# Layer norm transposes by DMA, from one SBUF tile to another, in place of TensorE

## The chip, the cores and the metric

The kernel runs on one core of a Trainium2 chip. The metric is the time on the device in microseconds (us), the median of several runs. One core has TensorE (in the profile PE, its weight loads PEld), VectorE (DVE), ScalarE (ACT), GpSimd (POOL) and SyncE (SP), and 16 DMA engines. DMAs are issued from the queues of SyncE and ScalarE.

## The reference

Two layers; each is a sliding-window attention block (32 heads of 32, a window of 8 keys two apart) and a gated MLP, with a layer norm before each block. All tensors are bfloat16, 2048 tokens of 1024.

```python
x = A_x
x = x + A(layernorm(x), A_wqkv, A_wo)         # q,k,v = x @ wqkv; 8 dilated keys per query; @ wo
x = x + B(layernorm(x), B_w1, B_w3, B_w2)     # (silu(x @ w1) * (x @ w3)) @ w2, inner size 3584
x = x + A(layernorm(x), A_wqkv, A_wo)
x = x + B(layernorm(x), B_w1, B_w3, B_w2)
```

## The kernel before

The tokens are cut into four chunks of 512. For each layer a chunk goes through a stage Q (layer norm, then q, k, v), two stages T (attention, nearly all on VectorE, with the `po` matmuls at the end) and a stage B (layer norm, then the MLP). The stages of different chunks are interleaved, so that TensorE works on B while VectorE works on T. A framework orders each engine's instructions when the program is built, from its own model of time. In the traces each engine keeps to that order: an instruction at the head of its queue that takes long delays all behind it.

The matmuls want the normalized rows with the feature dimension on partitions. So each layer norm of a chunk ends in transposes, 16 times in all (8 chunks for Q, 8 for B), with four row tiles each:

```python
    xnp = ctx.enter_context(tc.tile_pool(name="xn", bufs=2))
    psQ = ctx.enter_context(tc.tile_pool(name="psQ", bufs=2, space=PSUM))   # Q: two PSUM buffers
    psB = ctx.enter_context(tc.tile_pool(name="psB", bufs=4, space=PSUM))   # B: four
    # ... cut ...
    def ln_chunk(c, psum):
        with hp():                                     # high priority in the ordering
            # ... cut: statistics on VectorE, square root on ScalarE ...
            for j in range(TPC):                       # 4 row tiles of 128 x 1024
                xn = xnp.tile([P, D], BF16, name="xn")
                nc.vector.tensor_scalar(xn[:], x_sb[:, n, :], mv[:, j, 0:1], rstd[:, j:j + 1],
                                        op0=ALU.subtract, op1=ALU.mult)
                pT = psum.tile([P, KT, P], BF16, name="pT", tag="mm")
                for kk in range(KT):                   # 8 transposes of 128 x 128
                    nc.tensor.transpose(pT[:, kk, :], xn[:, kk * P:(kk + 1) * P], ident[:])
                nc.scalar.copy(xnT[:, :, j * P:(j + 1) * P], pT[:])
```

ScalarE also takes every result of Q out of PSUM, and applies silu to every gate of B:

```python
                    for kk in range(KT):               # Q: one PSUM buffer is filled in 8 matmuls
                        nc.tensor.matmul(ps[:], lhsT=w[:, kk, t::KT], rhs=xnT[:, kk, :], ...)
                    nc.scalar.copy(sgt[:, t - t0, :], ps[:])
                # ... cut; B:
                        nc.scalar.activation(sg[:], pg[:], ACTF.Silu)
                        nc.vector.tensor_tensor(hT[:, g0 + fi - f0, :], sg[:], pu[:], op=ALU.mult)
```

Of the kernel before, what the change touches and what calls it, by code (L numbers as in the profile page):

```python
# [15 lines left out]
def kernel(  # L16
# [13 lines left out]
    nc = tc.nc  # L30
    cfg = dict(cfg or {})
    P = 128
# [30 lines left out]
    const = ctx.enter_context(tc.tile_pool(name="const", bufs=1))  # L63
    wA = ctx.enter_context(tc.tile_pool(name="wA", bufs=2))
    wF = ctx.enter_context(tc.tile_pool(name="wF", bufs=4))
    xnp = ctx.enter_context(tc.tile_pool(name="xn", bufs=2))
    xtp = ctx.enter_context(tc.tile_pool(name="xnT", bufs=2))
    scr = ctx.enter_context(tc.tile_pool(name="scr", bufs=2))
    wk = ctx.enter_context(tc.tile_pool(name="wk", bufs=1))
# [6 lines left out]
    psQ = ctx.enter_context(tc.tile_pool(name="psQ", bufs=2, space=PSUM))  # L76
    psB = ctx.enter_context(tc.tile_pool(name="psB", bufs=4, space=PSUM))
# [22 lines left out]
    def hp(on=True):  # L100
        return tc.high_priority(offset=BOOST) if on else nullcontext()

    def ln_chunk(c, psum):
        with hp():
            xnT = xtp.tile([P, KT, CH], BF16, name="xnT")
            st = small.tile([P, TPC, 2, 6], FP32, name="st")
            mv = small.tile([P, TPC, 2], FP32, name="mv")
            for j in range(TPC):
                n = c * TPC + j
                for hh in range(2):  # L110
                    nc.vector.bn_stats(st[:, j, hh, :], x_sb[:, n, hh * 512:(hh + 1) * 512])  # L111
                nc.vector.bn_aggr(mv[:, j, :], st[:, j, :, :])
            sd = small.tile([P, TPC], FP32, name="sd")
            rstd = small.tile([P, TPC], FP32, name="rstd")
            nc.scalar.activation(sd[:], mv[:, :, 1], ACTF.Sqrt, bias=epst[:])
            nc.vector.reciprocal(rstd[:], sd[:])
            for j in range(TPC):
                n = c * TPC + j
                xn = xnp.tile([P, D], BF16, name="xn")
                nc.vector.tensor_scalar(xn[:], x_sb[:, n, :], mv[:, j, 0:1], rstd[:, j:j + 1],  # L120
                                        op0=ALU.subtract, op1=ALU.mult)
                pT = psum.tile([P, KT, P], BF16, name="pT", tag="mm")
                for kk in range(KT):
                    nc.tensor.transpose(pT[:, kk, :], xn[:, kk * P:(kk + 1) * P], ident[:])  # L124
                nc.scalar.copy(xnT[:, :, j * P:(j + 1) * P], pT[:])  # L125
        return xnT
# [6 lines left out]
    pending_ln = {}  # L133

    def q_stage(l, c, ln_next=None):
        xnT = pending_ln.pop((l, c), None)
        if xnT is None:
            xnT = ln_chunk(c, psQ)
        for which in range(3):
            w = wA.tile([P, KT, D], BF16, name="wqkv", tag="wA")  # L140
            nc.sync.dma_start(w[:], wqkv_v[:, :, which * D:(which + 1) * D])
            if l == 0 and c == 0:
                if which == 0 and NCH > 1:
                    nc.sync.dma_start(x_sb[:, TPC:2 * TPC, :], xin[:, TPC:2 * TPC, :])
                if which == 2:
                    for cc in range(2, NCH):
                        nc.sync.dma_start(x_sb[:, cc * TPC:(cc + 1) * TPC, :], xin[:, cc * TPC:(cc + 1) * TPC, :])
                    nc.sync.dma_start(wo[:], wo_v)
            for t0 in range(0, KT, SG):
                sgt = stg.tile([P, SG, CH], BF16, name="sgt")  # L150
                for t in range(t0, t0 + SG):
                    ps = psQ.tile([P, CH], FP32, name="ps", tag="mm")
                    for kk in range(KT):
                        nc.tensor.matmul(ps[:], lhsT=w[:, kk, t::KT], rhs=xnT[:, kk, :],  # L154
                                         start=(kk == 0), stop=(kk == KT - 1))
                    nc.scalar.copy(sgt[:, t - t0, :], ps[:])  # L156
                nc.sync.dma_start(qkv_d[l][which][:, t0:t0 + SG, c * CH:(c + 1) * CH], sgt[:])
            if which == 1 and ln_next is not None:
                pending_ln[ln_next] = ln_chunk(ln_next[1], psQ)

    def t_stage(l, tcx):
        tok0 = tcx * TCH
# [66 lines left out]
            nc.vector.tensor_tensor(xs, xs, ps[:].rearrange("p a b -> p (a b)"), op=ALU.add)  # L229

    def b_stage(c, last):
        xnT = ln_chunk(c, psB)
        for (f0, f1) in fsplits:
            for g0 in range(f0, f1, FG):
                gn = min(FG, f1 - g0)
                w1t = wF.tile([P, KT, FG * P], BF16, name="w1t", tag="wF")
                nc.sync.dma_start(w1t[:, :, 0:gn * P], w1_v[:, :, g0 * P:(g0 + gn) * P])
                w3t = wF.tile([P, KT, FG * P], BF16, name="w3t", tag="wF")
                nc.sync.dma_start(w3t[:, :, 0:gn * P], w3_v[:, :, g0 * P:(g0 + gn) * P])
                for fi in range(gn):  # L240
                    pg = psB.tile([P, CH], FP32, name="pg", tag="mm")
                    for kk in range(KT):
                        nc.tensor.matmul(pg[:], lhsT=w1t[:, kk, fi * P:(fi + 1) * P], rhs=xnT[:, kk, :],  # L243
                                         start=(kk == 0), stop=(kk == KT - 1))
                    pu = psB.tile([P, CH], FP32, name="pu", tag="mm")
                    for kk in range(KT):
                        nc.tensor.matmul(pu[:], lhsT=w3t[:, kk, fi * P:(fi + 1) * P], rhs=xnT[:, kk, :],  # L247
                                         start=(kk == 0), stop=(kk == KT - 1))
                    with hp():
                        sg = sgp.tile([P, CH], BF16, name="sg")  # L250
                        nc.scalar.activation(sg[:], pg[:], ACTF.Silu)  # L251
                        nc.vector.tensor_tensor(hT[:, g0 + fi - f0, :], sg[:], pu[:], op=ALU.mult)  # L252
            lastsplit = (f1 == fsplits[-1][1])
            for hh in range(2):
                w2ts = []
                for g0 in range(f0, f1, 8):
                    gn = min(8, f1 - g0)
                    w2t = wF.tile([P, 8, 512], BF16, name="w2t", tag="wF")
                    nc.sync.dma_start(w2t[:, 0:gn, :], w2_v[:, g0:g0 + gn, hh * 512:(hh + 1) * 512])
                    w2ts.append(w2t)  # L260
                for j in range(TPC):
                    n = c * TPC + j
                    acc = psB.tile([P, 512], FP32, name="acc", tag="mm")
                    for f in range(f0, f1):
                        nc.tensor.matmul(acc[:], lhsT=hT[:, f - f0, j * P:(j + 1) * P],  # L265
                                         rhs=w2ts[(f - f0) // 8][:, (f - f0) % 8, :],
                                         start=(f == f0), stop=(f == f1 - 1))
                    xs = x_sb[:, n, hh * 512:(hh + 1) * 512]
                    with hp():
                        nc.vector.tensor_tensor(xs, xs, acc[:], op=ALU.add)  # L270
                    if last and lastsplit:
                        nc.sync.dma_start(xout[:, n, hh * 512:(hh + 1) * 512], xs)
# [11 lines left out]
    for idx, (kind, l, c) in enumerate(stages):  # L284
        if kind == "Q":
            nxt = None
            if l == 0:
                for k2, l2, c2 in stages[idx + 1:idx + 2 + R]:
                    if k2 == "Q" and l2 == 0:
                        nxt = (l2, c2)  # L290
                        break
            q_stage(l, c, nxt)
        elif kind == "T":
            t_stage(l, c)
        else:
            b_stage(c, last=(l == 1))
# [30 lines left out]
```

## Time and profile before

| | before |
|---|---|
| time, median | 1697.18 us (1696.16 to 1697.53, 3 runs) |
| span of the profiled run | 1695.1 us |
| TensorE busy | 1653.8 us (98%) |
| VectorE / ScalarE busy | 1142.0 / 377.5 us |
| TensorE transposes | 512, 37.8 us busy |

The first lines are from the page. Behind an engine stand its busy time, its share of the span and its instructions; PEclk is the clock granted to TensorE in 40 slices, in tenths; q1 is SyncE's DMA queue, with packets, megabytes and share of the 16 engines' time.

```profile
span 1695.1 us, 19718 instructions
...
PE 1653.8 (98%) x7936; PEld 820.2 (48%) x7936; DVE 1142.0 (67%) x1926; ACT 377.5 (22%) x557; POOL 1.9 (0%) x12
...
PEclk9999999999999999999999999999999999999999
...
q1 hardware_dynamic: 282752, 288.25, 52.6%
```

The groups of instructions of the same page: line, engine, operation, tiles and shapes, count, then busy time, mean ns of one, idle time of the engine just before them, and what ended most of it.

```profile
L154 PE MATMUL ps<-xnT,wqkv 128*128 128x512 bf16 x1536 | 341.8, 382 | 5.8 <-ACT sgt L156 3.6
...
L225 PE MATMUL po<-wo,oT 128*128 128x512 bf16 x512 | 126.9, 380 | 7.7 <-DVE oT L131 6.6
L125 ACT COPY xnT<-pT 128x1024 bf16<-128x1024 bf16 x64 | 61.6, 1023 | 159.7 <-PE pT L124 155.0
...
L124 PE MATMUL pT<-ident,xn 128*128 128x128 bf16 x512 | 37.8, 225 | 23.4 <-DVE xn L120 20.7
```

The waits view (who waited for whom: us in total, times, longest).

```profile
PE pT L124 <- DVE xn L120: 20.7, 11, 11.7
...
PE po L225 <- DVE oT L131: 6.6, 13, 2.1
...
PE ps L154 <- ACT sgt L156: 3.6, 5, 1.8
```

One line of TensorE's timeline (start, duration), just before a Q stage of the second layer: sixteen transposes in 1.06 us.

```profile
917.38 1.06 PE L124 MATMUL pT<-ident,xn 128*128 128x128 bf16 x16
```

And the windows view for the first 250 us, in which most of layer 0's Q chunks fall. It is used as a clock later on: TensorE executed 1124 matmuls, 160 of them transposes, so 964 useful ones. (Busy time and count of each engine, then the granted clock, the DMA share and GB/s.)

```profile
core 0: us, PE busy (x) PEld busy (x) DVE busy (x) ACT busy (x) POOL busy (x), PEclk, DMA share, GB/s
0.00:250.00 250.00, 226.94 (x1124) 139.27 (x1125) 207.60 (x366) 87.51 (x135) 1.89 (x12) 0.99 0.73 245
```

### The profile page before, as it was taken

The numbers are of one execution on the slowest core, as the hardware profiler recorded it, in microseconds if no ns is written. First come the engines' busy times: TensorE is split into PE (matmuls) and PEld (weight loads), VectorE is DVE, ScalarE is ACT, GpSimd is POOL, SyncE is SP. The second block draws the span as 40 slices with busy tenths as digits, with TensorE's granted clock in tenths as the row PEclk, the third lists the DMA queues.
The fourth block names the chain that finished last, engine by engine and source line by source line (L and its number), as shares of the span: only waits on it lengthen the run. The fifth ranks groups of instructions, "written<-read, shape, count | busy, mean of one in ns | idle before, by whom it ended". The sixth has DMA issues, their size and how long they took to land.

```text
span 1695.1 us, 19718 instructions
## 1 busy us (share of the span) xinstructions
PE 1653.8 (98%) x7936; PEld 820.2 (48%) x7936; DVE 1142.0 (67%) x1926; ACT 377.5 (22%) x557; POOL 1.9 (0%) x12
## 2 busy tenths in 40 slices
PE   6999999999999999999999999999999999999999
PEld 4655644444444444564445644455444554444444
DVE  5599999999997822229982299823997159952212
ACT  3333422112212111132012320223212231121100
POOL 0000000000000000000000000000000000000000
PEclk9999999999999999999999999999999999999999
DMA  8975656553553344575344764357543555436442
GB/s 298 316 263 187 205 176 188 171 163 115 176 162 127 98 153 156 166 240 179 125 136 149 237 187 126 124 180 244 175 141 108 183 165 165 149 103 195 149 149 99
DMA packets 282843, 289.51 MB, mean 171 GB/s; under 512 B 6144, under 2 KB 256000, under 8 KB 282624
## 3 DMA queue, kind: packets, MB, share of 16 engines
q1 hardware_dynamic: 282752, 288.25, 52.6%
q8 instruction: 62, 1.02, 0.2%
q14 instruction: 29, 0.24, 0.0%
HBM read 258.87 MB, written 29.36 MB: 170 GB/s over the span
## 4 chain that ended last, share of the span: by engine, by line
PE 49%; DVE 42%; issue 4%; DMA 3%; ACT 2%; SPq 0%; DVEq 0%; ACTq 0%
PE acc L265 15%; PE pu L247 11%; PE pg L243 10%; PE ps L154 10%; DVE pr L177 6%; DVE tm L218 6%; DVE hT L252 4%; DVE pr L129 4%; PE po L225 3%; DVE tm L129 3%; DVE st L111 3%; DVE pr L130 2%; DVE tm L130 2%; DMA qkv_d_1_134<-sgt 2%; DVE x_sb L270 1%
## 5 line engine op out<-in xcount | busy, mean ns | idle before, releaser
L247 PE MATMUL pu<-xnT,w3t 128*128 128x512 bf16 x1792 | 429.9, 379 | 0.0
L243 PE MATMUL pg<-xnT,w1t 128*128 128x512 bf16 x1792 | 429.4, 379 | 0.3 <-ACT xnT L125 0.3
L265 PE MATMUL acc<-w2t,hT 128*128 128x512 bf16 x1792 | 392.7, 379 | 0.8 <-DVE hT L252 0.8
L154 PE MATMUL ps<-xnT,wqkv 128*128 128x512 bf16 x1536 | 341.8, 382 | 5.8 <-ACT sgt L156 3.6
L251 ACT ACTIVATE sg<-pg 128x512 bf16<-128x512 f32 x224 | 133.7, 597 | 676.9 <-PE pg L243 663.8
L154 PEld LDWEIGHTS <-wqkv 128*128 128x128 bf16 x1536 | 220.1, 144 | 120.2 <-issue 12.4
L265 PEld LDWEIGHTS <-hT 128*128 128x128 bf16 x1792 | 174.9, 98 | 209.6 <-DVE hT L252 1.5
L243 PEld LDWEIGHTS <-w1t 128*128 128x128 bf16 x1792 | 175.2, 98 | 208.2 <-issue 0.8
L247 PEld LDWEIGHTS <-w3t 128*128 128x128 bf16 x1792 | 175.2, 98 | 207.5
L177 DVE TENSOR_TENSOR pr<-qT,kT 128x2048 bf16<-128x2048 bf16 x128 | 154.0, 1217 | 170.8 <-DMA kT<-qkv_d_1_134 156.9
L252 DVE TENSOR_TENSOR hT<-sg,pu 128x512 bf16<-128x512 bf16 x224 | 152.4, 680 | 168.5 <-PE pu L247 160.4
L270 DVE TENSOR_TENSOR x_sb<-x_sb,acc 128x512 bf16<-128x512 bf16 x128 | 87.2, 682 | 147.6 <-PE acc L265 147.6
L156 ACT CAST sgt<-ps 128x512 bf16<-128x512 f32 x192 | 111.9, 585 | 229.4 <-PE ps L154 202.2
L218 DVE TENSOR_TENSOR tm<-At,vT 128x2048 bf16<-128x2048 bf16 x128 | 152.9, 1217 | 0.1
L225 PE MATMUL po<-wo,oT 128*128 128x512 bf16 x512 | 126.9, 380 | 7.7 <-DVE oT L131 6.6
L125 ACT COPY xnT<-pT 128x1024 bf16<-128x1024 bf16 x64 | 61.6, 1023 | 159.7 <-PE pT L124 155.0
L225 PEld LDWEIGHTS <-oT 128*128 128x128 bf16 x512 | 48.8, 97 | 89.8 <-DVE oT L131 39.3
L129 DVE TENSOR_TENSOR pr<-pr 128x1024 bf16<-128x1024 bf16 x128 | 86.4, 681 | 0.0
L129 DVE TENSOR_TENSOR tm<-tm 128x1024 bf16<-128x1024 bf16 x128 | 84.7, 684 | 0.0
L111 DVE BATCH_NORM_STATS2 st<-x_sb 128x6 f32<-128x512 bf16 x128 | 80.7, 672 | 4.7 <-DMA x_sb<-in_A_x_dram 4.4
L124 PE MATMUL pT<-ident,xn 128*128 128x128 bf16 x512 | 37.8, 225 | 23.4 <-DVE xn L120 20.7
L229 DVE TENSOR_TENSOR x_sb<-x_sb,po 128x1024 bf16<-128x1024 bf16 x32 | 38.8, 1212 | 24.5 <-PE po L225 24.4
(175 smaller groups left out, 511.2 us busy)
## 6 DMA issues: line engine op xcount, KB each, us to landing
w1t<-in_B_w_dram SPq DMA_DIRECT2D x56, 1024.0 KB, 5.4
w3t<-in_B_w_dram SPq DMA_DIRECT2D x56, 1024.0 KB, 7.4
wqkv<-in_A_wqkv_dram SPq DMA_DIRECT2D x24, 2048.0 KB, 9.0
w2t<-in_B_w_dram SPq DMA_DIRECT2D x48, 1024.0 KB, 5.5
w2t<-in_B_w_dram SPq DMA_DIRECT2D x16, 512.0 KB, 5.3
qkv_d_0_130<-sgt SPq DMA_DIRECT2D x16, 256.0 KB, 5.1
qkv_d_1_131<-sgt SPq DMA_DIRECT2D x16, 256.0 KB, 5.5
qT<-qkv_d_0_130 SPq DMA_DIRECT2D x8, 512.0 KB, 4.7
```

The source lines that it names most:

```text
L111: nc.vector.bn_stats(st[:, j, hh, :], x_sb[:, n, hh * 512:(hh + 1) * 512])
L129: nc.vector.tensor_tensor(buf[:, 0:4, :], buf[:, 0:4, :], buf[:, 4:8, :], op=ALU.add)
L154: nc.tensor.matmul(ps[:], lhsT=w[:, kk, t::KT], rhs=xnT[:, kk, :], start=(kk == 0), stop=(kk == KT - 1))
L156: nc.scalar.copy(sgt[:, t - t0, :], ps[:])
L177: nc.vector.tensor_tensor(pr[:], qT[:], kT[:, :, k0:k0 + TCH], op=ALU.mult)
L218: nc.vector.tensor_tensor(tm[:], At[:], win, op=ALU.mult)
L225: nc.tensor.matmul(ps[:, hh, :], lhsT=oT[:, t, j * P:(j + 1) * P], rhs=wo[:, t, hh * 512:(hh + 1) * 512], start=(t == 0), stop=(t == KT - 1))
L243: nc.tensor.matmul(pg[:], lhsT=w1t[:, kk, fi * P:(fi + 1) * P], rhs=xnT[:, kk, :], start=(kk == 0), stop=(kk == KT - 1))
L247: nc.tensor.matmul(pu[:], lhsT=w3t[:, kk, fi * P:(fi + 1) * P], rhs=xnT[:, kk, :], start=(kk == 0), stop=(kk == KT - 1))
L251: nc.scalar.activation(sg[:], pg[:], ACTF.Silu)
L252: nc.vector.tensor_tensor(hT[:, g0 + fi - f0, :], sg[:], pu[:], op=ALU.mult)
L265: nc.tensor.matmul(acc[:], lhsT=hT[:, f - f0, j * P:(j + 1) * P], rhs=w2ts[(f - f0) // 8][:, (f - f0) % 8, :], start=(f == f0), stop=(f == ...
```

## The change

The intent: TensorE is the limit, and transposes do no arithmetic, so let the DMA engines do them. A DMA transpose reads `xn` and writes `xnT` directly, without PSUM and without ScalarE's eviction (the copy out of PSUM). ScalarE's queue issues it: the issue is an instruction of ScalarE that starts the DMA, and the DMA has landed when all its data is in place. Only the first chunk, on whose layer norm everything waits, stays on TensorE. One more `xn` buffer covers the longer life of a tile.

```diff
-    xnp = ctx.enter_context(tc.tile_pool(name="xn", bufs=2))
+    xnp = ctx.enter_context(tc.tile_pool(name="xn", bufs=3))
@@ ln_chunk
+                if psum is None:
+                    nc.scalar.dma_start_transpose(out=xnT[:, :, j * P:(j + 1) * P], in_=xn[:])
+                    continue
                 pT = psum.tile([P, KT, P], BF16, name="pT", tag="mm")
@@ q_stage
-            xnT = ln_chunk(c, psQ)
+            xnT = ln_chunk(c, psQ if (l, c) == (0, 0) else None)
...
-                pending_ln[ln_next] = ln_chunk(ln_next[1], psQ)
+                pending_ln[ln_next] = ln_chunk(ln_next[1], None)
@@ b_stage
-        xnT = ln_chunk(c, psB)
+        xnT = ln_chunk(c, None)
```

## The prediction

> **What bounds the kernel now.** TensorE. The page's busy table gives PE 1653.8 us of a span of 1695.1 (98%); the granted clock is 0.999. Start to start (timeline view) the 512-column matmuls follow each other every 216 ns (128 acc matmuls in 27.6 us), so the 7,424 useful ones need 1603.6 us. The other 91 us: 11.7 before the first PE instruction, 3.6 after the last matmul, 42 of transposes (512, start to start 81 ns each, gaps included; 37.8 by the groups table), 8 of gaps just before transposes, the rest waits for buffers and VectorE, 16 of them before the po matmuls (their oT comes from VectorE, 97 to 100% busy from 100 to 500 us in the windows view).
>
> **Removed.** 480 of 512 PE transposes and their weight loads: on PE 480 x 81 ns = 39 us, plus some 6 us of waits before and between them (PE waiting for xn, 20.7 us by the waits view, mostly at the start, which stays). Also 60 ScalarE evictions of 1.02 us (ScalarE is 22% busy: worth nothing directly) and pT's turns in the PSUM pools.
>
> **Added.** 60 DMA transposes of 256 KB, 15.7 MB on top of 289.5 MB (5%). The Trainium skill, "DMA: Bandwidth & Descriptors", section "Latency and other measured facts", gives 261 GB/s for a transpose with a non-contiguous middle dimension: 1.0 us of data, an estimate. No run here shows a transpose yet; plain 256 KB stores in this trace land 3.3 to 5.5 us after issue, so I expect 3 to 6 us to land, some 15 us for a chunk's four, with only three xn buffers. Each holds ScalarE's queue while issued: SyncE's plain issues take 0.37 to 0.67 us; I estimate 1 us, what the eviction took.
>
> **Moved.** Transposes no longer wait for PSUM or PE. In the second layer the first two xn of a Q chunk are ready 20 to 100 us before they are transposed (893 against 917 us): most landing time will be hidden. xn[3] must wait for xn[0]'s landing, and VectorE works in order: waits of 1 to 3 us per chunk.
>
> **How much is critical.** Nearly all of the PE time removed, since PE is the limit: at most 45 us. I give back: in 100 to 500 us VectorE is as full as PE, so the 96 transposes there (about 10 us) mostly become longer waits of po for oT; elsewhere a few us of queue waits. Net gain 30 to 40 us.
>
> **Prediction.** 1661 us (-2.1%), 8 in 10 between 1643 and 1692. Faster by over 2%: 0.52; within 2%: 0.38; slower by over 2%: 0.10.
>
> **What would show it.** Right: PE busy about 1618 us; pT only 32 transposes; no PE wait longer than 2 us on xnT's DMA after the first chunk; po's waits grow by 5 to 10 us; DMA share up 1 to 4 points; ScalarE busy down about 60 us; no PE wait for weights.
>
> **What would make it wrong.** (a) The transpose is several times slower than the estimate, or slows the loads beside it: then PE waits for weights or xnT. (b) Issuing it, or waiting for xn, holds ScalarE's queue for several us: sg and sgt evictions come late, and with two PSUM buffers in Q and four in B, PE stops after 2 to 4 us; its issue times would show that. (c) VectorE stops for the third or fourth xn buffer in the T stage. (d) The new order of instructions places po worse or better: 10 us either way, unrelated to the transposes' cost.

## The result, and the profile after

The changed kernel is correct and takes 1717.37 us (1715.94 to 1718.16, 4 runs), against 1696.82 us (1696.16 to 1697.53) of the kernel before beside it. The ratio is 1.012, with a 95% interval of 1.0106 to 1.0134. Here and below, a ratio is the mean time of one kernel's fast runs over that of the other's fast runs of the same rounds, so it is not quite the ratio of the medians quoted. The change makes the kernel 20.5 us (1.2%) slower; 36 us faster was predicted.

| | before | after |
|---|---|---|
| span of the profiled run | 1695.1 us | 1716.0 us |
| TensorE busy | 1653.8 us | 1634.3 us |
| TensorE waits for ScalarE's `sgt` | 3.6 us | 30.7 us |
| VectorE waits for a landing, to reuse `xn` | none | 74.6 us |
| transposes on TensorE | 512 | 32 |

The page's lines after (q10 is ScalarE's DMA queue):

```profile
span 1716.0 us, 18813 instructions
...
PE 1634.3 (95%) x7456; PEld 795.2 (46%) x7456; DVE 1142.5 (67%) x1926; ACT 326.7 (19%) x502; POOL 1.9 (0%) x12
...
PEclk9898999999999999999999999999999999999999
...
q1 hardware_dynamic: 282752, 288.25, 52.7%
q10 hardware_dynamic: 63360, 15.74, 5.0%
```

The groups that answer to those of before, and the one that makes `xn`:

```profile
L246 PE MATMUL pg<-xnT,w1t 128*128 128x512 bf16 x1792 | 431.5, 380 | 11.5 <-ACT sg L254 11.5
...
L157 PE MATMUL ps<-xnT,wqkv 128*128 128x512 bf16 x1536 | 346.3, 387 | 31.8 <-ACT sgt L159 30.7
...
L228 PE MATMUL po<-wo,oT 128*128 128x512 bf16 x512 | 127.9, 380 | 15.5 <-DVE oT L134 12.2
...
L120 DVE TENSOR_SCALAR xn<-x_sb,mv,rstd 128x1024 bf16<-128x1024 bf16 x64 | 32.9, 543 | 75.3 <-DMA xnT<-xn 74.6
```

TensorE has 480 instructions fewer and is still later. Its idle time before the `ps` matmuls of stage Q (L157, formerly L154) rose from 5.8 to 31.8 us, and ScalarE's eviction ended nearly all of it. The clock dips in slices of the first 250 us. The waits view gives the same names, and a new one, VectorE waiting for the DMA that still reads an `xn` buffer:

```profile
DVE xn L120 <- DMA xnT<-xn: 74.6, 22, 7.6
...
PE ps L157 <- ACT sgt L159: 30.7, 6, 10.5
...
PE po L228 <- DVE oT L134: 12.2, 13, 1.9
...
PE pg L246 <- ACT sg L254: 11.5, 6, 4.0
```

What holds ScalarE? The view of the tile `xnT` shows the issues themselves (minimum, median and maximum ns that one held the queue) and the time to landing:

```profile
L123 ACTq DMA_TRANSPOSE xnT<-xn x60: 1246/1329/6813, 24.0 to 1532.3; - x60
...
DMA to landing us min/median/max: 3.1/6.4/11.9
```

An issue holds ScalarE's queue for 1.25 us at the least and 6.81 us at the most. Of the 60, 24 take over 2 us, mostly the second and third of a chunk; the first of a chunk never does (1.25 to 1.33 us in all 15), even where its own DMA lands only 11.9 us later. In the trace all 60 sum up to 139.7 us. ScalarE's timeline at the layer norm of the third chunk shows what that does:

```profile
66.75 0.58 ACT L159 CAST sgt<-ps 128x512 bf16<-128x512 f32 x1 [2.14 <-DMA qkv_d_2_132<-sgt]
67.47 11.62 ACTq L123 DMA_TRANSPOSE xnT<-xn  x3
79.14 1.07 ACT L159 CAST sgt<-ps 128x512 bf16<-128x512 f32 x2 [11.81 <-DMA xnT<-xn]
79.94 1.31 ACTq L123 DMA_TRANSPOSE xnT<-xn  x1
```

Three transposes are issued in a row and hold the queue from 67.47 to 79.09 us (1.25, 6.81 and 3.50 us). Their `xn` tiles had been written before, so it is not VectorE that ScalarE waits for. For 11.8 us no PSUM buffer is emptied. TensorE meanwhile:

```profile
65.77 3.51 PE L157 MATMUL ps<-xnT,wqkv 128*128 128x512 bf16 x15
79.78 5.71 PE L157 MATMUL ps<-xnT,wqkv 128*128 128x512 bf16 x13 [10.50 <-ACT sgt L159]
```

It fills what buffers it has, stops for 10.50 us, and then does 13 matmuls in 5.71 us, where the 15 ahead of the stop took 3.51. The granted clock has dropped to half (0.51 in the windows view of these 5.71 us, the third figure from the end):

```profile
79.78:85.49 5.71, 5.71 (x14) 2.30 (x14) 5.45 (x13) 1.02 (x2) 0.00 (x0) 0.51 0.68 165
```

The Trainium skill, "TensorE: Matmul & The Clock Gate", section "Why this matters for your kernels", tells to avoid idle gaps of more than about 3 us for that reason; this trace agrees, with the 10.50 us stop and the doubled spacing behind it. But half the clock also came after shorter stops: for 3.41 us from 515.43 us, just after one of 1.99 us, and in the kernel before for 3.41 us from 154.37 us, just after one of 2.03 us.

The windows view tells where in time the loss arises:

```profile
0.00:250.00 250.00, 204.45 (x901) 124.03 (x902) 179.37 (x316) 69.98 (x115) 1.89 (x12) 0.93 0.80 250
```

In the first 250 us TensorE executed 901 matmuls, 869 of them useful, where the kernel before had done 964. The 95 that are missing are 20.5 us of TensorE at 216 ns, as much as the whole loss. From 250 us to the end both kernels need the same time for a useful matmul: (1695.1 - 250) / (7424 - 964) = 223.7 ns before, and (1716.0 - 250) / (7424 - 869) = 223.6 ns after. So two things have to be explained: a loss of 20 us at the start, and a gain that fails to come in the rest. In the rest the largest new wait is that of B's gate matmuls, `pg`, for ScalarE's silu, `sg` (11.5 us; none before): at 776.48 us, for example, three transposes of a Q chunk hold ScalarE for 10.22 us while a B stage runs, and TensorE stops for 4.04 us.

A third reading sums it up. I added up, over all neighbouring matmuls of the trace, the start-to-start time beyond 216 ns (beyond 55 ns after a transpose): the time TensorE loses to waits, stops and the slow clock. It is 48.2 us before and 94.8 us after. The transposes removed are 480 x 55 ns = 26.4 us, and 94.8 - 48.2 - 26.4 = 20.2 us is the slowdown.

### The profile page after: what moved, and what is told of

Its sections match the earlier page's. It is cut to its first block, busy times and chain, and to the rows that moved or that the text cites. A ratio compares the mean times of both kernels' runs of the same rounds, so it can differ in the third digit from the quotient of the medians.

```text
span 1716.0 us, 18813 instructions
## 1 busy us (share of the span) xinstructions
PE 1634.3 (95%) x7456; PEld 795.2 (46%) x7456; DVE 1142.5 (67%) x1926; ACT 326.7 (19%) x502; POOL 1.9 (0%) x12
## 3 DMA queue, kind: packets, MB, share of 16 engines
q1 hardware_dynamic: 282752, 288.25, 52.7%
q10 hardware_dynamic: 63360, 15.74, 5.0%
## 4 chain that ended last, share of the span: by engine, by line
PE 40%; DVE 24%; DMA 4%; issue 3%; ACT 1%; ACTq 1%; DVEq 0%; SPq 0%
PE acc L268 12%; PE pu L250 10%; PE pg L246 10%; PE ps L157 6%; DVE pr L180 4%; DVE tm L221 3%; DVE hT L255 3%; PE po L228 3%; DVE pr L132 2%; DVE tm L132 2%; DMA qkv_d_1_134<-sgt 2%; DVE st L111 1%; DMA xnT<-xn 1%; DVE x_sb L273 1%; DVE pr L133 1%
## 5 line engine op out<-in xcount | busy, mean ns | idle before, releaser
L246 PE MATMUL pg<-xnT,w1t 128*128 128x512 bf16 x1792 | 431.5, 380 | 11.5 <-ACT sg L254 11.5
L157 PE MATMUL ps<-xnT,wqkv 128*128 128x512 bf16 x1536 | 346.3, 387 | 31.8 <-ACT sgt L159 30.7
L157 PEld LDWEIGHTS <-wqkv 128*128 128x128 bf16 x1536 | 221.5, 144 | 153.8 <-issue 47.3
L228 PE MATMUL po<-wo,oT 128*128 128x512 bf16 x512 | 127.9, 380 | 15.5 <-DVE oT L134 12.2
L120 DVE TENSOR_SCALAR xn<-x_sb,mv,rstd 128x1024 bf16<-128x1024 bf16 x64 | 32.9, 543 | 75.3 <-DMA xnT<-xn 74.6
L133 DVE TENSOR_TENSOR pr<-pr 128x512 bf16<-128x512 bf16 x128 | 52.5, 414 | 0.2
```

What stands on the lines that cost most here:

```text
L228: nc.tensor.matmul(ps[:, hh, :], lhsT=oT[:, t, j * P:(j + 1) * P], rhs=wo[:, t, hh * 512:(hh + 1) * 512], start=(t == 0), stop=(t == KT - 1))
L246: nc.tensor.matmul(pg[:], lhsT=w1t[:, kk, fi * P:(fi + 1) * P], rhs=xnT[:, kk, :], start=(kk == 0), stop=(kk == KT - 1))
```

## The experiments

Theories. **H**: an issue that finds earlier DMAs still queued holds ScalarE's in-order queue for several us; evictions come late and TensorE stops, above all in Q with its two PSUM buffers. **B**: the cost is VectorE's waits for an `xn` buffer. **O**: the cost is the new order of instructions. Later on, **HC** is H with its cause: the earlier DMAs are the loads in flight; **HB** would hold any second transpose in a row. A caution for all runs: the order is made anew for each build, on every engine, so no edit changes one thing alone. Line numbers shift by a few between kernels.

| run | transposes | time, us | ratio to before (95%) |
|---|---|---|---|
| changed kernel | DMA from ScalarE | 1717.37 | 1.012 (1.0106 to 1.0134) |
| e1_sp | DMA from SyncE | 1674.91 | 0.9872 (0.9853 to 0.989) |
| e1b_sp, the same again | DMA from SyncE | 1674.24 | 0.9873 (0.9853 to 0.9894) |
| e2_bufs5 | from ScalarE, 5 xn buffers | 1712.94 | 1.0095 (1.008 to 1.011) |
| e3_sp_bufs5 | from SyncE, 5 xn buffers | 1678.53 | 0.9892 (0.9877 to 0.9906) |
| e4_actcopy (wrong result) | none, ScalarE copies | 1673.28 | 0.9859 (0.9844 to 0.9874) |
| e5_plaindma (wrong result) | plain DMA from ScalarE | 1721.73 | 1.0155 (1.014 to 1.017) |
| e6_before_light (wrong result) | TensorE, less VectorE work | 1684.11 | 0.9929 (0.9912 to 0.9945) |
| e7_actcopy_light (wrong result) | e4, less VectorE work | 1658.93 | 0.9785 (0.9768 to 0.9801) |
| e8_act_bonly | B from ScalarE, Q on TensorE | 1683.6 | 0.9927 (0.9908 to 0.9946) |
| e9_sp_hybrid | from SyncE, layer 0's Q on TensorE | 1676.76 | 0.9886 (0.9869 to 0.9904) |
| e10_none (wrong result) | none at all | 1664.7 | 0.9816 (0.9798 to 0.9833) |
| e11_after_resident (wrong result) | from ScalarE, fewer loads | 1674.46 | 0.9865 (0.9848 to 0.9882) |
| e12_before_resident (wrong result) | TensorE, fewer loads | 1691.94 | 0.9964 (0.9945 to 0.9983) |

### The issuing queue: e1_sp

```diff
-                    nc.scalar.dma_start_transpose(out=xnT[:, :, j * P:(j + 1) * P], in_=xn[:])
+                    nc.sync.dma_start_transpose(out=xnT[:, :, j * P:(j + 1) * P], in_=xn[:])
```

> Only edit: the 60 transposes are issued from SyncE instead of ScalarE. Theory H (hold): a transpose issued right behind another holds ScalarE's queue for 4 to 7 us (seen in the changed kernel's trace: 1.25 us for the first of a burst, 4.1 to 6.8 us for the second), PSUM evictions wait behind it and TensorE stops. H expects PE's wait for ScalarE's sgt (30.7 us in the changed kernel) under 8 us and a time of 1665 to 1680 us. Rival B (buffers): VectorE's 74.6 us of waits for a free xn buffer delay oT; expects 1705 to 1720 us here, because landings are no sooner. Rival O (order): only the new order of instructions costs; expects no systematic change, 1700 to 1725 us.

The result is correct, and one word is worth 42 us: 1674.91 us. This kernel is faster than both. Its view of `xnT`, its waits and its first 250 us:

```profile
L123 SPq DMA_TRANSPOSE xnT<-xn x60: 1231/1310/4218, 22.0 to 1489.8; - x60
...
DMA to landing us min/median/max: 3.0/4.2/9.2
```

```profile
DVE xn L120 <- DMA xnT<-xn: 21.5, 18, 2.8
PE ps L157 <- ACT sgt L159: 14.7, 5, 7.3
...
PE po L228 <- DVE oT L134: 11.3, 15, 1.9
```

```profile
0.00:250.00 250.00, 219.35 (x998) 132.60 (x999) 209.76 (x369) 72.34 (x119) 1.89 (x12) 0.97 0.84 262
```

TensorE's wait for `sgt` is halved (14.7 us; under 8 was expected, so H was somewhat too bold), and after 250 us TensorE has done 998 - 32 = 966 useful matmuls, level with the kernel before. From 250 us on a useful matmul takes (1672.8 - 250) / (7424 - 966) = 220.3 ns instead of 223.6, so the gain in the rest has come too. The lost time, summed as above, is 52.3 us instead of 94.8. The issues are shorter too (4.22 us at most), perhaps because SyncE issues no loads while it is held by a transpose, which no run tests: so this run alone doesn't tell whether ScalarE being held, or the meeting with loads, is the root. B and O both fail here, as neither expected a change of this size.

### The buffers: e2_bufs5 and e3_sp_bufs5

Tiles `psm` and `At` share one buffer to make room for two more of `xn`. e3 has the edit of e1 as well.

```diff
-    xnp = ctx.enter_context(tc.tile_pool(name="xn", bufs=3))
+    xnp = ctx.enter_context(tc.tile_pool(name="xn", bufs=5))
...
-        psm = wk.tile([P, W, TCH], BF16, name="psm")
+        psm = wk.tile([P, W, TCH], BF16, name="psm", tag="pa")
...
-        At = wk.tile([P, W, TCH], BF16, name="At")
+        At = wk.tile([P, W, TCH], BF16, name="At", tag="pa")
```

> Five xn buffers instead of three (psm and At share one buffer to make room), transposes still from ScalarE. Rival B expects VectorE's wait for landings to fall from 74.6 us to under 15 us and the time to 1690 to 1705 us. Theory H expects that wait to fall too, but the time to stay within 8 us of 1717 us or to rise, as four transposes then stand in the queue in a row and hold ScalarE longer.

> Both: issued from SyncE, five xn buffers. If H is the main cost and B the second one: 1655 to 1670 us, faster than e1_sp by 5 to 12 us. If B is nothing: equal to e1_sp within 4 us.

The waits of e2_bufs5:

```profile
PE ps L157 <- ACT sgt L159: 34.1, 5, 10.6
...
DVE xn L120 <- DMA xnT<-xn: 28.8, 7, 8.5
```

VectorE's wait fell from 74.6 to 28.8 us (B had expected under 15), and the time by 4 us; TensorE's wait for `sgt` stayed. From SyncE the extra buffers gain nothing (1678.53 us). B is no more than a few us. The large number in the waits view was mostly slack.

### The value of the transposes: e4_actcopy, e6, e7 and e10_none

The edit of e4 (against the changed kernel) leaves the data untransposed:

```diff
-                    nc.scalar.dma_start_transpose(out=xnT[:, :, j * P:(j + 1) * P], in_=xn[:])
+                    nc.scalar.copy(xnT[:, :, j * P:(j + 1) * P], xn[:].rearrange("p (k t) -> p k t", k=KT))
```

> Wrong result on purpose: no transposes at all, ScalarE copies xn into xnT (from SBUF, about 1 us, as the eviction before took). It shows what taking the transposes off TensorE is worth with no DMA in its place. H and B expect 1650 to 1662 us (the 45 us of the prediction's ideal). O expects 1685 us or more, since the order changes here as well.

It takes 1673.28 us, 23 us under the kernel before and not 45. O, which expected 1685 us or more, fails here too. The prediction had also mis-sized the prize. The lost time of its trace is 49.1 us, against 48.2 before: TensorE lost the 26.4 us of transposes, and none of the gaps. I first blamed VectorE (theory V), since the waits of `po` for `oT` grew from 6.6 to 15.0 us, and took work off it, in a pair:

```diff
     def tree_sum8(buf, dst):
-        nc.vector.tensor_tensor(buf[:, 0:4, :], buf[:, 0:4, :], buf[:, 4:8, :], op=ALU.add)
-        nc.vector.tensor_tensor(buf[:, 0:2, :], buf[:, 0:2, :], buf[:, 2:4, :], op=ALU.add)
```

> Wrong result on purpose: the kernel before with two of the three adds of tree_sum8 left out, which takes some 275 us of work off VectorE in the T stages. Partner of e7. Theory V (VectorE kept the kernel without transposes from gaining more than 23 us): this kernel is 1665 to 1690 us, since PE stays the limit, and e7 is 33 to 45 us faster than it. Rival (the gaps around the transposes were never worth anything): e7 is only 20 to 28 us faster.

> Wrong result on purpose: e4_actcopy (no transposes, ScalarE copies) with the same two adds left out. V expects 1633 to 1648 us, 33 to 45 us under e6_before_light; the rival expects 20 to 28 us under it.

The pair differs by 1684.11 - 1658.93 = 25.2 us, as the rival said and about as much as without the edit. V falls: with a fifth of VectorE's busy time gone (909.2 us in e6, 1142.0 before), the transposes are worth no more. For the upper bound, e10 drops even the copy, and reads a constant tile (not shown: the tile's creation, and one `xnT` buffer instead of two):

```diff
-            xnT = xtp.tile([P, KT, CH], BF16, name="xnT")
+            xnT = xtp.tile([P, KT, CH], BF16, name="xnT") if psum is not None else xnT_c
...
-                    nc.scalar.dma_start_transpose(out=xnT[:, :, j * P:(j + 1) * P], in_=xn[:])
```

> Wrong result on purpose: no transposes, no DMA and no copy; after the first chunk the matmuls read a constant tile, and the normalized rows are computed and dropped. It shows the most that taking the transposes off TensorE can give. The prediction's sum (39 us of transposes and 6 us of gaps around them) expects 1650 to 1655 us. If the gaps only move to other places, as e4 against before says (26 us of transposes themselves, and no fewer gaps): 1664 to 1672 us.

1664.7 us, 30 us under the kernel before. That is all the transposes were worth, with nothing in their place and with no matmul after the first chunk waiting for a layer norm. With the transposes issued from SyncE, 21 of these 30 us are had (1694.95 - 1674.24, e1b_sp, on the same chip as e10).

### What makes an issue long: m1_micro and e5_plaindma

A kernel of its own, whose phases wait for all of the phase before; each has four moves of a 128 x 1024 tile in a row.

```python
    phase("A", nc.scalar, True, 0)    # queue, transpose?, four 1 MB loads from SyncE in flight?
    phase("B", nc.scalar, True, 1)
    phase("C", nc.scalar, False, 0)
    phase("D", nc.scalar, False, 2)
    phase("E", nc.sync, True, 0)
    phase("F", nc.sync, True, 2)
```

> Wrong result on purpose: six phases one after the other, each with four 256 KB moves in a row on otherwise idle engines. A: transposes from ScalarE, nothing else in flight. B: the same with four 1 MB loads from SyncE in flight. C, D: plain copies of the same tiles from ScalarE, without and with the loads. E, F: transposes from SyncE, alone, and issued behind the four loads. Theory HC (the hold comes from competing with loads in flight): in A each issue takes 1.2 to 1.6 us and lands in about 3 us; in B the second or third is held 4 us or more and the first lands after 6 us or more; F is held as B is. Rival HB (a second transpose in a row is always held): A shows 4 us for the second issue as well. For C and D: if the hold belongs to transposes only, every plain issue takes under 0.8 us in both; if it belongs to any DMA of 1,024 pieces of 256 B, D shows holds of several us too.

Its timeline gives for each phase the time from the first issue to the end of the fourth:

```profile
28.30 5.52 ACTq L65 DMA_TRANSPOSE dA<-sA  x4
...
37.48 12.89 ACTq L65 DMA_TRANSPOSE dB<-sB  x4
...
57.86 3.38 ACTq L67 DMA_DIRECT2D dC<-sC  x4
...
66.22 9.69 ACTq L67 DMA_DIRECT2D dD<-sD  x4
...
88.00 5.44 SPq L65 DMA_TRANSPOSE dE<-sE  x4
...
102.01 11.37 SPq L65 DMA_TRANSPOSE dF<-sF  x4
```

| phase | each issue, us | to landing, us (min, median, max) |
|---|---|---|
| A: transposes, ScalarE, alone | 1.34 to 1.36 | 3.2, 3.4, 3.4 |
| B: the same beside loads | 1.40, 4.07, 3.53, 3.60 | 7.7, 9.8, 11.4 |
| C: plain copies, ScalarE, alone | 0.66, 0.63, 0.67, 1.14 | 3.0, 3.8, 4.3 |
| D: the same beside loads | 0.60, 0.98, 3.94, 3.88 | 9.7, 12.9, 15.8 |
| E: transposes, SyncE, alone | 1.28 to 1.31 | 3.2, 3.2, 3.3 |
| F: the same behind the loads | 5.85, 2.70, 1.26, 1.29 | 3.2, 4.0, 9.7 |

HC is right and HB wrong: four transposes in a row hold nothing while the DMA engines are free (5.52 us for the four, and the last landed 3.2 us after its issue), and 12.89 us beside loads. F is held as well, but only in its first two issues, not as B is. And the hold is no property of transposes: plain copies in the same small pieces are held nearly as long in D. "Advanced Engine Details and Errata", section "X-Bar Transpose (TRN2)", of the Trainium skill says that "TRN2 transpose DMAs are as fast as regular DMAs"; A against C agrees in the landing (3.4 against 3.8 us at the median), while the issue takes twice as long (1.35 against 0.66 us).

The same in the kernel, as the only edit against the changed one:

```diff
-                    nc.scalar.dma_start_transpose(out=xnT[:, :, j * P:(j + 1) * P], in_=xn[:])
+                    nc.scalar.dma_start(xnT[:, :, j * P:(j + 1) * P], xn[:].rearrange("p (k t) -> p k t", k=KT))
```

> Wrong result on purpose: in the changed kernel each of the 60 transposes is a plain DMA copy of the same 256 KB in pieces of 256 B, from ScalarE still. If the hold belongs to the transpose instruction: plain issues under 0.8 us each, PE's wait for sgt under 12 us, time 1672 to 1685 us. If any DMA of that many pieces holds the queue when loads are in flight: issues of 3 us and more, time 1700 to 1720 us.

```profile
L123 ACTq DMA_DIRECT2D xnT<-xn x60: 601/634/8302, 23.7 to 1541.7; - x60
...
DMA to landing us min/median/max: 2.9/7.7/14.0
```

1721.73 us, no faster than with transposes, and TensorE waits 33.6 us for `sgt`. The median issue is short (0.63 us), but one in four takes over 2 us, up to 8.3. Their sum, 91.9 us, is smaller than the transposes' 139.7, at no smaller a loss: this suggests that what counts is not the sum but the longest holds, those that outlast the two PSUM buffers.

### The dose: e8_act_bonly and e9_sp_hybrid

```diff
-            xnT = ln_chunk(c, psQ if (l, c) == (0, 0) else None)      # e8
+            xnT = ln_chunk(c, psQ)
...
-                pending_ln[ln_next] = ln_chunk(ln_next[1], None)      # e8 and e9
+                pending_ln[ln_next] = ln_chunk(ln_next[1], psQ)
...
-            xnT = ln_chunk(c, psQ if (l, c) == (0, 0) else None)      # e9, with nc.sync as in e1
+            xnT = ln_chunk(c, psQ if l == 0 else None)
```

> Dose of the hold: only the eight B chunks (32 transposes) go by DMA from ScalarE; the eight Q chunks stay on TensorE. B has four PSUM buffers where Q has two, so it should bear a hold of 4 us better. Theory HC expects PE's wait for sgt to fall from 30.7 us to under 8 us, no clock drop in the first 150 us beyond the one of the kernel before, and a time between 1680 and 1698 us. If the loss were spread over all transposes evenly, half of it would stay: 1702 to 1712 us.

> Candidate: transposes by DMA from SyncE, except the four Q chunks of layer 0, which stay on TensorE, because there the DMA engines are 90% busy and SyncE's stores of q, k, v then come late (PE stops of 7.4 and 2.9 us in e1_sp). Expected 1665 to 1676 us, up to 6 us faster than e1b_sp; if the stops at the start cost no more than the transposes they replace, equal to it within 3 us.

TensorE's wait for `sgt` in e8_act_bonly:

```profile
PE ps L157 <- ACT sgt L159: 5.5, 5, 2.9
```

With DMA transposes from ScalarE for B alone, the change is a gain: 1683.6 us, 0.9927 of the kernel before. The wait for `sgt` is down to 5.5 us, and none for `sg` is left, though it is B's transposes that stayed on ScalarE. Most of the harm came with the transposes of the Q chunks; only one of the four long stops of the changed kernel in the first 250 us (5.64 us, ended at 217.02 us) came with those of a B chunk, while a Q stage still ran. e9 was to improve on e1 and doesn't: 1676.76 us against 1674.24 us on the same chip, equal within the intervals. TensorE's stop of 7.3 us (e1_sp, in the waits above) is gone, its longest wait for `sgt` is now 2.0 us, and its transposes are back.

### The loads, in the kernel: e11 and e12

e1 changes two things at once, and m1_micro is not the kernel. So the loads were taken away instead: the weights of Q are loaded once and used for all three products (e11 on the changed kernel, e12 on the one before; not shown: the pool `wA` shrinks from two buffers to one in both).

```diff
-            w = wA.tile([P, KT, D], BF16, name="wqkv", tag="wA")
-            nc.sync.dma_start(w[:], wqkv_v[:, :, which * D:(which + 1) * D])
+            if "w" not in w_res:
+                w_res["w"] = wA.tile([P, KT, D], BF16, name="wqkv", tag="wA")
+                nc.sync.dma_start(w_res["w"][:], wqkv_v[:, :, 0:D])
+            w = w_res["w"]
```

> Wrong result on purpose: the changed kernel (transposes from ScalarE), but the weights of the Q stages are loaded once, and all three products use them, which takes 46 MB of loads away from the Q stages. Theory HC (the holds come from loads in flight, in the kernel as in m1_micro): fewer issues held over 2 us than the 24 of the changed kernel (under 12), PE's wait for sgt under 12 us, and a time at least 5 us under e12_before_resident. If the loads are not the cause in the kernel: holds and PE's wait as in the changed kernel, and 15 to 25 us slower than e12_before_resident.

> Wrong result on purpose: partner of e11, the kernel before with the weights of the Q stages loaded once. No DMA wait holds PE in the kernel before, so both theories expect 1685 to 1700 us.

```profile
L123 ACTq DMA_TRANSPOSE xnT<-xn x60: 1246/1296/4326, 25.3 to 1490.1; - x60
...
DMA to landing us min/median/max: 3.0/3.8/8.9
```

```profile
PE ps L160 <- ACT sgt L162: 11.1, 4, 3.3
```

The transposes are still issued from ScalarE, and now the change wins by 1691.94 - 1674.46 = 17.5 us, where it lost 20.5 with the loads. Ten issues instead of 24 take over 2 us, none of them in the first 300 us (6 of the 24 were there), and TensorE's wait for `sgt` is 11.1 us instead of 30.7. e12, the kernel before with the same edit, takes 4.4 us less than without it (1696.36 us in the same rounds). So HC holds in the kernel too: ScalarE's queue is held because loads are in flight. The order of instructions is new in both kernels, so the holds and waits of the traces are evidence for this as much as the times are. The loads alone don't do it, though: a first issue of a chunk is never held (above, and 1.40 us in phase B). All 24 long issues of the changed kernel found an earlier transpose of the same queue that had not landed. In phase A an earlier transpose alone lengthened nothing either (1.34 to 1.36 us). In these runs it takes both.

Why do loads in flight lengthen an issue that much? The transposes move in pieces of 15.74 MB / 63,360 = 248 bytes on average, SyncE's DMAs, mostly loads, in 288.25 MB / 282,752 = 1,019 bytes. The Trainium skill, "DMA: Bandwidth & Descriptors", section "Queues, rings and completion order", says that each DMA engine takes turns between its queues by packet. If each turn moves as many pieces of one queue as of the other, a transpose gets about a fifth of the bytes beside a load (an estimate from these sizes), and its queue drains slowly. The trace of m1_micro agrees. In phase B, from 42 to 52 us, both queues have work, and the DMA view of that window counts (packets, MB, share of the DMA engines):

```profile
q1 hardware_dynamic: 2749, 2.78, 82.1%
q10 hardware_dynamic: 2730, 0.68, 31.8%
```

As many packets of the transposes (q10) as of the loads (q1), and 0.68 of 3.46 MB, a fifth: 68 GB/s, where the transposes of phase A, alone, move 0.57 MB from 30 to 33 us, 191 GB/s. The landings fit (9.8 us beside loads against 3.4 alone). Nor is it that ScalarE waits for SyncE's issues: in phase B the last of these ended at 42.42 us, and ScalarE's third and fourth issue, from 43.15 and 46.77 us, still took 3.53 and 3.60 us. Left open is how much must stand in a queue before the next issue is held: no run varies the piece size, or the number or spacing of the issues. Also open is how much of e1b_sp's distance from e10 on the same chip (1674.24 - 1664.7 = 9.5 us) is order and how much is contention.

## Why the prediction was wrong

- **What bounds the kernel**: right. TensorE was and stayed the limit (98% busy before, 95% after).
- **"Each holds ScalarE's queue while issued ... I estimate 1 us, what the eviction took"**: this is the step that failed. The median was 1.33 us, close enough, but 24 of 60 issues took 2.2 to 6.8 us, mostly the second and third of three in a row, in a queue that also empties PSUM. Point (b) of what could go wrong named the mechanism and where to see it; I gave it too little weight, because I took SyncE's plain issues (0.37 to 0.67 us) as typical for a queue that competes with those very loads. The trace before already held the warning: 6 of SyncE's 384 issues took 1.8 to 6.0 us, all in the first 120 us, and three of them were stores of `sgt`, 256 KB as a transpose is. Moving the issue to SyncE gave back 42 us (e1_sp), taking the loads away turned the loss into a gain of 17.5 us (e11 against e12).
- **"Nearly all of the PE time removed ... at most 45 us"**: mis-sized. With nothing in place of the transposes the kernel gains 30 us (e10), with a copy 23 (e4). I charged 81 ns for a transpose and 6 us of waits around them, gaps included. The gaps are waits that turn up elsewhere: lost time was 48.2 us before and 49.1 in e4. In e4 only the 55 ns from one transpose to the next, 26.4 us, was really removed.
- **"3 to 6 us to land"**: the median was 6.4 us, the maximum 11.9; alone it is 3.2 to 3.4 (m1_micro), at 191 GB/s, not at the 261 that the prediction took.
- **"waits of 1 to 3 us per chunk"** of VectorE: 74.6 us, 5 per chunk; but they cost only a few us (e2).
- **"po's waits grow by 5 to 10 us"**: right, 6.6 to 12.2 us in the changed kernel. That VectorE was why gains shrink there was not borne out by e6 and e7.
- **PE busy 1618 us, ScalarE down 60 us, DMA share up 1 to 4 points**: 1634.3 us (matmuls at half clock are busy for longer), down 51 us, up 5 points. That no PE wait for weights would come up, and none over 2 us for the DMA of `xnT`, was right.

## What to carry to other kernels

A DMA issue is an instruction of the engine that issues it: before you put one into the queue of an engine that empties PSUM, ask what will be in flight at that moment, and read the longest issue in the trace rather than the median. Where you can, put DMAs that meet other traffic on a queue on which nothing urgent waits; here that one word turned 20 us lost into 21 us gained. And when you count what removing an instruction from the busiest engine is worth, count its start-to-start pace first: here the gaps around it moved elsewhere.

## What the Trainium skill lacked or had wrong

- "DMA: Bandwidth & Descriptors", section "Issuing engines are not separate DMA queues", says that issuing from several engines only saves the time to initiate a DMA, "which is usually small relative to the DMA itself". Here the choice of the issuing engine was worth 42 us of 1717: an issue of 0.6 to 1.4 us took 3.5 to 4.1 us beside loads in m1_micro (phases B and D) and up to 6.8 (transposes) or 8.3 us (plain copies) in the kernel, and held its engine for so long. No page I read gives how much longer an issue gets beside other DMAs in flight.
- No page gives a measured issue time of a DMA transpose of this size on this chip; it would belong to "DMA: Bandwidth & Descriptors". The runs show 1.23 us at the least for a 128 x 1024 tile (1.25 from ScalarE), 1.28 to 1.36 us alone, against 0.63 to 0.67 us for most plain copies of it.
- "VectorE: DVE Perf Modes", section "The three transpose paths", gives 1309 ns for a 128 x 128 transpose by DMA. For eight times as much, 128 x 1024, these runs show 3.2 to 3.4 us from issue to landing on free engines, and 7.7 to 11.4 us beside loads, which the page doesn't mention.
- "TensorE: Matmul & The Clock Gate", section "Part 4: PE-mode transpose", gives about 275 ns for a transpose in one kernel's context. Here the record of one has 219 ns at the median, but sixteen in a row start 56 ns apart, and that pace is what removing them is worth.
